# Products with a recurrent state on four tiles of TensorE at once, and a new written-out order

## The chip, the core and the metric

The kernel runs on one core of a Trainium2 chip. Its engines work side by side, each through its own queue in order: TensorE (PE; its weight loads stand apart as PEld), VectorE (DVE), ScalarE (ACT), GpSimd (POOL), and SyncE (SP), which issues nearly all DMAs. The metric is device time in microseconds: the median of three runs. A profiled execution is a further one, and has a time of its own.

## The reference

A linear attention with decay, then two MLP blocks, for 2 batches, 8 heads of 48 and 768 tokens:

```python
for t in range(S):
    cur = np.einsum('bhd,bhe->bhde', u[None] * kt, vt)
    y[:, :, t] = np.einsum('bhd,bhde->bhe', rt, state + cur)
    state = wt[:, :, :, None] * state + np.einsum('bhd,bhe->bhde', kt, vt)

h = gelu(x @ w_in);  u, v = split(h);  v_n = layernorm(v) * g_ln
x = x + (u * (w_sg @ v_n + b_sg)) @ w_out

xk, xr = mixes of x and x of the token before, by mu_k and mu_r
out = sigmoid(xr @ w_r) * (relu(xk @ w_k) ** 2 @ w_v)
```

The weights of the MLPs come as 64-bit floats.

## The kernel before

**Attention.** The recurrence is cut into chunks of 64 tokens. A *unit* is one batch, one half of the sequence (384 tokens, six chunks) and one pair of heads: 16 units, of which 0 to 3 and 8 to 11 are first halves of the sequence. A pair's heads lie on partitions 0 to 47 and 64 to 111. Per unit the code makes, in this order as the data needs it:

- `scores` (token A, line 346) and `sums` (P, 354) into `pA`; `turn` (T, 333), a transpose of the keys, and `keys` (k, 337 and 339), which copies them back;
- `weigh` (m, 385) and `now` (n, 391) on VectorE: masked scores and the part of the current token;
- `states` (S, 363) into `pkv`, and `fade` (x): ScalarE copies them to `kv` (373), VectorE runs a scan over the chunks into `sx` (377);
- `inner` (J, 400) and `inject` (N, 406) into `py`, then `outer` (I, 413), the products of `r` with the states, into the same `py`;
- `store` (O, 418 or 421): ScalarE copies `py` to `xT`, or to `t1` for the last pair, which `share` (o) spreads by DMA.

These products have a depth of 64 or 48 and 64 or 48 columns, a quarter of TensorE's array. Which quarter a product takes follows from the partitions of its operands (the row half) and of its output (the column half). The loops run over `QUAD`, head h and parity q of the chunk, in the order (0,0), (1,1), (0,1), (1,0). In `scores` the row half goes with h and the column half with q; in `states`, `inner` and `inject` the other way round, so each set of four has four different quarters. In `outer` both go with h: there are two quarters for four products. Each of these products is of type f32 and stands as two rows in the trace. The tiles `pA` and `pkv` share one buffer, and `py` has one.

The states of a unit lie in `sx` as `[112, 48, 7]`, chunk last, so that one state's 48 columns are seven words apart; a second half's first state comes as a packed copy, `sl` (380).

**MLP.** Products of full size in three terms of high and low parts (`mm3`, lines 209 to 211): v, u, M, W, E, R, Z in the order, with `xsplit` (X), `gate` (G) and `mix` (Y) between. Weights (tokens C) are converted by VectorE in three integer steps (156, 161, 165) and split by ScalarE (168) and VectorE (177). `packs` (L, D, j, g, d, K, f) prepare decays on VectorE (271 to 288).

**Order.** Nothing is scheduled by a program: `ORDER` is a text of tokens, and each issues its instructions on all queues at once, DMAs too. Token e (line 654) issues a product that computes nothing, "idle". The attention ends at token `|`.

Of the kernel before, what the change touches and what calls it, by code (L numbers as in the profile page):

```python
# [43 lines left out]
n5 g5 C1.o d5 C1.q C2.h k5 O4 S5.0 J5 N5 S5.1 S5.2 e x5.0 K5 T6 A6 I5 P6 o3 o3 o3 C3.l w6 63 64 w7 65 X0.1.h X0.2.h C2.r X0.0.h C2.q O5 f5 k6 X0.2.l
C3.x C2.o C4.x v0.2 n6 m6 C3.b X0.1.l S6.0 S6.1 J6 N6 S6.2 X0.0.l C3.t C4.b L6 x6.0 D6 T7 v0.1 A7 P7 I6 C4.r v0.2 C3.h C3.o C4.t C4.q k7 v0.1 C3.r O6
C4.h C3.q C5.l m7 C5.x n7 C5.b C5.t j6 w8 q6 C5.h v0.0 S7.0 S7.1 J7 N7 S7.2 C4.o C5.o u0.0 u0.3 g6 K6 d6 C6.l C6.h x7.0 v0.2 q7 C15.l C15.h w9 L7 u0.0
f6 L8 q8 A8 P8 I7 D7 m8 n8 j7 g7 K7 d7 T8 O7 k8 C5.r v0.2 u0.3 J8 N8 S8.0 S8.1 S8.2 x8.0 u0.1 T9 A9 P9 I8 u0.2 o7 o7 o7 q10 67 C7.l w10 v0.0 v0.1 v0.0
O8 k9 D8 C6.o m9 j8 n9 g8 K8 X1.0.h X1.0.l d8 C15.o S9.0 J9 S9.1 N9 S9.2 X1.1.h v1.0 f7 X1.1.l x9.0 T10 A10 P10 I9 X1.2.h C7.h u0.2 v0.1 C5.q v0.0
v0.0 O9 n10 L9 D9 m10 C7.o X1.2.l j9 g9 v0.0 q9 d9 C8.l 68 66 v1.1 k10 u0.1 f8 v0.1 C8.h v0.2 S10.0 J10 S10.1 N10 S10.2 x10.0 v0.2 f9 v1.0 u1.1 T11
A11 P11 I10 w11 n11 K9 m11 v0.1 k11 v1.1 O10 L10 w12 B v1.0 v1.1 u1.3 J11 N11 S11.0 S11.1 S11.2 D10 j10 x11.0 g10 d10 L11 C11.l C9.l C11.h v1.0 v1.0  # L50
v1.0 K10 v1.2 A12 I11 P12 T12 v1.2 O11 C9.h u1.1 k12 u1.2 u1.2 v1.1 v1.1 m12 C11.o n12 C8.o J12 S12.0 S12.1 N12 S12.2 C13.l w13 C10.l q11 x12.0 u1.0
T13 A13 P13 I12 v1.2 C10.h v1.2 C9.o D11 n13 v1.1 O12 v1.2 u1.0 k13 j11 C10.o m13 v1.2 o11 g11 C24.l C24.x K11 M0.3 M0.3 J13 S13.0 N13 S13.1 S13.2
M0.0 o11 o11 X2.2.h X2.2.l x13.0 d11 X2.0.h C16.l C16.h C13.h C16.o M0.0 M0.0 C13.o A14 P14 I13 T14 w14 C19.l M0.3 n14 M0.2 w15 610 69 O13 X2.1.h k14
X2.1.l X2.0.l C19.x m14 C19.r C19.q C17.l 611 J14 N14 S14.0 S14.1 S14.2 C19.b C19.t M0.2 x14.0 v2.1 T15 I14 A15 P15 C14.l C14.h C14.o n15 m15 C24.r
f11 O14 k15 f10 v2.1 C17.h C24.q v2.0 J15 S15.0 N15 S15.1 S15.2 M0.1 C24.b C17.o C24.t M0.2 C12.l C12.h C12.o x15.0 M0.1 I15 v2.1 v2.2 C21.l O15 C21.r
u1.3 C21.q v2.2 v2.1 v2.0 | C19.h C24.h M1.0 M1.0 M1.0 C24.o M1.3 M1.2 v2.0 C20.l C18.l C18.r C18.q C19.o C21.x C20.x C20.b M0.1 C20.t C20.h C20.o
C21.b M1.1 C21.t C21.h v2.2 C18.x M1.3 C21.o C18.b C18.t C18.h M1.2 M1.2 C18.o M1.1 v2.0 v2.0 v2.1 v2.0 u2.0 u2.0 G0.0.h C25.l v2.1 C25.x G0.0.l C25.b
v2.2 C26.l C26.x o15 o15 o15 u2.1 u2.1 v2.2 G0.1.h v2.2 C20.r G0.2.h u2.3 u2.2 C22.l G0.3.h G0.1.l M1.1 C26.b G0.2.l u2.2 X3.0.h C20.q X3.2.h u2.3
G0.3.l C25.t W0.0 W0.0 C26.t X3.0.l C25.h C25.o X3.1.h C22.x C22.b X3.1.l C26.r C26.q C22.r C22.q W0.1 C25.r C26.h v3.0 W0.2 C22.t W0.1 X3.2.l W0.2
C26.o C34.l C27.l v3.0 v3.0 C25.q v3.2 C22.h v3.2 v3.1 M1.3 C27.x u3.1 v3.2 C35.l v3.0 v3.0 v3.1 u3.1 u3.3 u3.0 u3.2 v3.1 C27.b C27.t C27.h v3.2 C22.o  # L60
v3.2 C34.x C34.b u3.3 v3.0 v3.2 C27.o C34.t v3.1 C34.r C28.l G1.2.h u3.0 v3.1 v3.1 C34.q G1.0.h u3.2 C34.h C27.r C27.q C35.x C35.b M2.3 G1.2.l M2.3
C35.t C35.h C35.o M2.2 M2.2 M2.2 C31.l C28.r G1.3.h G1.3.l C28.q M2.1 M2.0 C31.r G1.1.h G1.0.l G1.1.l C31.q C35.r C34.o C31.x C31.b C31.t C35.q C31.h
M2.3 C28.x C28.b C28.t C28.h M2.0 C31.o W1.1 M2.1 C23.l C29.l C36.l W1.1 M2.0 M2.1 C28.o C29.x C29.b W1.2 W1.0 W1.0 G2.1.h G2.0.h F C29.r C29.q C29.t
C23.x C23.b C29.h C23.t C23.h C23.o C36.x C37.l M3.0 M3.1 G2.3.h C36.r C36.q C37.r M3.0 G2.3.l G2.0.l C29.o M3.1 C37.x C37.q G2.2.h G2.2.l M3.0 M3.1
C37.b M3.3 M3.2 M3.3 H0 G2.1.l Y0.0.0.a W1.2 M3.2 Y0.0.2.a Y0.0.1.a Y0.1.1.a M3.3 C36.b C37.t C37.h Y0.0.0.b Y0.0.1.b W2.2 W2.2 W2.0 W2.1 Y0.0.2.b
Y0.1.0.a C36.t G3.0.h C23.r Y0.1.0.b C23.q Y0.1.1.b Y0.0.0.c Y0.0.2.c Y0.0.1.c C37.o W2.1 W2.0 C38.l C38.x C30.l C32.l E0.1 G3.3.h M3.2 Y0.1.0.c E0.0
E0.0 E0.1 C38.b C38.t E0.1 E0.2 C38.h C36.h C38.r C38.o E0.0 E0.0 E0.1 E0.1 E0.0 E0.3 E0.3 E0.2 C36.o E0.6 Z0.0 C33.l Y0.1.2.a E0.2 Y0.1.2.b C33.x
Y0.1.2.c Y0.1.1.c C30.x C30.b C30.t C33.b E0.2 C30.h E0.3 E0.3 C38.q E0.2 C33.t E0.3 E0.6 E0.6 E0.6 C30.o C32.x G3.3.l E0.5 R0.0 Z0.1 E0.4 E0.4 E0.4
E0.4 E0.7 G3.1.h C32.b C32.t C32.h C33.h C32.r C32.q Z0.2 R0.2 Z0.3 E0.4 E0.6 C33.o C32.o Z0.4 E0.7 E0.5 E0.5 R0.0 H1 Y1.0.0.a Y1.0.0.b E0.5 Y1.0.1.a
E0.5 Y1.0.0.c Y1.0.2.a E0.7 R0.1 R0.1 Z0.5 Z0.6 Y1.1.0.a Y1.0.1.b Y1.0.1.c C30.r Y1.1.0.b E0.7 Y1.0.2.b Y1.0.2.c E1.0 E1.0 C30.q Y1.1.1.a E0.7 E1.0  # L70
G3.1.l G3.0.l Y1.1.2.a C33.r C33.q G3.2.h E1.2 E1.2 Y1.1.1.b Y1.1.2.b R0.2 Z0.7 z0.0 E1.0 Y1.1.1.c E1.2 E1.2 E1.2 E1.4 E1.5 E1.1 E1.5 G3.2.l Y1.1.2.c
E1.0 Y1.1.0.c E1.5 E1.3 E1.5 E1.3 H2 E1.5 z0.1 E1.3 z0.2 E1.1 Y2.0.0.a E1.1 E1.3 E1.1 E1.1 y0.0 y0.2 y0.1 R1.1 R1.0 E1.4 E1.4 E1.4 E1.4 E1.6 E1.6 R1.0
R1.2 W3.1 Z1.0 E1.7 E1.3 W3.1 Y2.0.0.b Y2.0.0.c E1.6 Y2.0.2.a Y2.0.1.a Y2.1.1.a Y2.1.0.a R1.2 E1.7 Y2.1.0.b Y2.0.1.b Y2.0.2.b E1.6 R1.1 E1.7 E1.7
Y2.0.1.c W3.0 Z1.1 Z1.2 Z1.3 Z1.4 Y2.1.0.c E1.6 Y2.1.2.a Y2.1.2.b E1.7 Y2.1.1.b Y2.1.2.c Z1.5 Z1.6 Y2.1.1.c Y2.0.2.c E2.0 E2.0 E2.2 E2.2 E2.2 E2.0
W3.0 E2.3 Z1.7 E2.0 z1.1 E2.0 E2.3 E2.3 z1.2 E2.3 z1.0 W3.2 W3.2 E2.3 E2.5 E2.1 E2.1 E2.2 E2.2 E2.4 E2.5 E2.5 E2.1 E2.1 E2.5 H3 Y3.0.0.a Y3.0.2.a E2.5
y1.2 y1.0 y1.1 R2.0 E2.6 E2.7 E2.6 E2.6 E2.1 E2.4 E2.6 E2.6 Y3.0.0.b Y3.0.2.b E2.7 Y3.0.1.a E2.7 Y3.0.1.b Y3.0.1.c E2.4 Y3.1.2.a Y3.0.0.c R2.2 Z2.0
E2.7 R2.0 R2.2 E2.4 E2.4 Z2.1 Z2.2 Z2.3 Z2.4 Z2.5 Y3.1.0.a Y3.0.2.c Y3.1.1.a E3.1 R2.1 E3.0 Y3.1.0.b E3.0 Y3.1.1.b E3.2 Z2.6 Y3.1.1.c E2.7 E3.3 E3.0
Z2.7 E3.3 E3.3 E3.0 z2.0 R2.1 E3.3 E3.6 E3.0 Y3.1.0.c Y3.1.2.b z2.1 Y3.1.2.c R3.1 E3.3 E3.2 E3.2 E3.2 E3.1 E3.1 E3.1 z2.2 E3.2 E3.1 y2.0 y2.2 y2.1
E3.5 E3.4 R3.0 E3.4 E3.6 E3.4 E3.6 E3.6 E3.4 R3.0 E3.4 R3.2 R3.2 E3.5 E3.6 R3.1 E3.5 E3.5 E3.5 E3.7 E3.7 E3.7 E3.7 E3.7 Z3.0 Z3.2 z3.2 z3.0 Z3.1 y3.2
# [853 lines left out]
```

## Time and profile before

| | |
|---|---|
| median of 3 runs | 335.76 us (335.6 to 336.11) |
| profiled execution | 336.34 us, its span 334.4 us |
| TensorE, weight loads | 319.8 us (96%), 296.3 us (89%) |
| VectorE, ScalarE, GpSimd | 239.5, 182.3, 44.3 us |
| instructions | 8994 |
| HBM over the span | 81 GB/s |

The span is the time from the first to the last instruction that the profiler saw. Busy shares are sums over the whole span, which has stages of different kinds. Ends of matmuls are modelled and overlap the next ones, so what a group of products costs is read from its start to the start of the next group, its slot. "issue" names time in which an engine waited for nothing that the profile shows.

### The profile page before, as it was taken

How to read it: one execution, taken by the hardware profiler on the slowest of the kernel's cores; microseconds unless marked ns; L12 is line 12 of the kernel's file. 1: busy time of each engine (PE TensorE's matmuls, PEld its weight loads, DVE VectorE, ACT ScalarE, POOL GpSimd, SP SyncE). 2: the span in 40 equal slices, each digit the busy share in tenths (PEclk: the TensorE clock that was granted, in tenths of full speed). 3: DMA queues.
4: the chain of work that ended last, by engine and by line, in shares of the span. 5: the costliest groups of instructions: out<-in, count | busy, mean ns of one | idle time of the engine just before them, and what ended most of it. 6: DMA issues, size and time to landing. Idle time of an engine off the chain costs nothing.

```text
span 334.4 us, 8994 instructions
## 1 busy us (share of the span) xinstructions
PE 319.8 (96%) x3734; PEld 296.3 (89%) x3734; DVE 239.5 (72%) x451; ACT 182.3 (54%) x432; POOL 44.3 (13%) x98
## 2 busy tenths in 40 slices
...
GB/s 207 233 211 142 100 222 163 146 143 168 119 153 93 162 149 20 70 136 156 4 95 159 47 0 144 47 2 0 25 49 0 0 2 71 2 0 24 49 0 76
DMA packets 16509, 30.00 MB, mean 90 GB/s; under 512 B 2256, under 2 KB 12496, under 8 KB 16464
## 3 DMA queue, kind: packets, MB, share of 16 engines
...
q14 instruction: 15, 0.12, 0.1%
...
## 4 chain that ended last, share of the span: by engine, by line
PE 78%; DMA 4%; DVE 2%; ACT 2%; SPq 2%; issue 1%; DVEq 0%; ACTq 0%
PE po L575 11%; PE pk L210 5%; PE pk L209 5%; PE pk L211 5%; PE ps L209 5%; PE ps L211 5%; PE ps L210 5%; PE po L211 4%; PE po L210 4%; PE po L209 4%; PE pu L209 2%; PE py L413 2%; PE pu L211 2%; PE pu L210 2%; PE pv L209 2%; PE pr L211 2%
## 5 line engine op out<-in xcount | busy, mean ns | idle before, releaser
L209 PE MATMUL ps<-wsg,vn_hi 128*128 128x384 f32 x96 | 32.7, 340 | 0.0
L210 PE MATMUL pk<-xk_lo,wk_hi 128*128 128x384 f32 x96 | 32.6, 339 | 0.0
L211 PE MATMUL ps<-wsg,vn_lo 128*128 128x384 f32 x96 | 32.4, 337 | 0.1
L209 PE MATMUL pk<-xk_hi,wk_hi 128*128 128x384 f32 x96 | 32.5, 338 | 0.0
L211 PE MATMUL pk<-xk_hi,wk_lo 128*128 128x384 f32 x96 | 32.4, 338 | 0.0
L210 PE MATMUL ps<-wsg,vn_hi 128*128 128x384 f32 x96 | 32.3, 336 | 0.0
L547 ACT ACTIVATE kr<-pk 128x384 f32<-128x384 f32 x32 | 15.3, 490 | 26.4 <-PE pk L211 20.0
L549 DVE TENSOR_TENSOR kr<-kr 128x384 f32<-128x384 f32 x32 | 17.5, 555 | 16.0 <-ACT kr L547 15.8
L556 DVE TENSOR_TENSOR kk_lo<-kr,kk_hi 128x384 fp32r<-128x384 f32 x32 | 17.3, 554 | 9.3 <-ACT kk_hi L554 9.3
L554 ACT CAST kk_hi<-kr 128x384 fp32r<-128x384 f32 x32 | 16.0, 511 | 14.3 <-DVE kr L549 10.9
L575 PE MATMUL po<-pl_win_hi,kk_hi 128*128 128x384 f32 x81 | 22.8, 336 | 0.0
L377 DVE TENSOR_TENSOR_SCAN sx<-kv,fd 112x336 f32<-112x336 f32 x16 | 13.7, 855 | 7.8 <-ACT kv L373 7.3
L211 PEld LDWEIGHTS ps<-wsg,vn_lo 128*128 128x128 f32 x96 | 18.0, 188 | 0.4 <-DVE vn_lo L479 0.4
L209 PEld LDWEIGHTS ps<-wsg,vn_hi 128*128 128x128 f32 x96 | 18.0, 188 | 0.3
L575 PE MATMUL po<-pl_win_lo,kk_hi 128*128 128x384 f32 x63 | 18.2, 336 | 0.0
L210 PEld LDWEIGHTS pk<-xk_lo,wk_hi 128*128 128x128 f32 x96 | 18.0, 188 | 0.2 <-DVE xk_lo L538 0.2
L575 PE MATMUL po<-pl_win_hi,kk_lo 128*128 128x384 f32 x54 | 18.2, 337 | 0.0
L209 PEld LDWEIGHTS pk<-xk_hi,wk_hi 128*128 128x128 f32 x96 | 18.0, 188 | 0.1
L210 PEld LDWEIGHTS ps<-wsg,vn_hi 128*128 128x128 f32 x96 | 18.1, 188 | 0.0
L211 PEld LDWEIGHTS pk<-xk_hi,wk_lo 128*128 128x128 f32 x96 | 18.0, 188 | 0.0
L209 PE MATMUL pu<-xs_hi,win_hi 128*128 128x384 f32 x48 | 16.8, 351 | 0.0
L211 PE MATMUL po<-ga_hi,wout_lo 128*128 128x384 f32 x48 | 16.2, 337 | 0.0
...
## 6 DMA issues: line engine op xcount, KB each, us to landing
...
wsg_raw<-in_w_sgT_dram SPq DMA_DIRECT2D x12, 192.0 KB, 3.0
out_dram<-rr SPq DMA_DIRECT2D x12, 192.0 KB, 1.9
...
```

The lines of the kernel that those rows point to most:

```text
L209: T.matmul(ps, lh, rh, start=(i == 0), stop=False)
L210: T.matmul(ps, lh, rl, start=False, stop=False)
L211: T.matmul(ps, ll, rh, start=False, stop=(i == n - 1))
L377: V.tensor_tensor_scan(u.sx.rearrange(flat), u.kv.rearrange(flat), u.fd.rearrange(flat), 0.0, ALU.add, ALU.mult)
L413: T.matmul(u.py[o:o + D, q, c * CA:(c + 1) * CA], u.state(n)[o:o + D, :], u.rp[o:o + D, n * CA:(n + 1) * CA], start=False, stop=(c == NCB ...
L547: A.activation(kr, ps, AF.Relu)
L549: V.tensor_mul(kr, kr, kr)
L554: A.copy(hi, kr)
L556: V.tensor_sub(lo, kr, hi.bitcast(F32))
L575: T.matmul(pv[g][s], l, wv[i][r], start=st, stop=(i == KF - 1 and l is ll))
```

## The change

Outputs of `inner`, `inject` and `outer` go to the column half `h ^ q` in place of h. Chunks of odd parity so stand in the other half of `py`'s partitions, and the four products of `outer` take four different quarters; `inner` and `inject` keep four. `store` becomes three copies: even chunks of both heads (112 x 192), and odd chunks of each head (48 x 192) with the halves exchanged. `ORDER` is new throughout; it has 68 idle tokens in place of 44, 57 of them ahead of unit 7's states in place of 44, two ahead of unit 10's `turn`, and nine behind the last product of all.

```diff
-... L2 q2 C0.l w1 g1 m0 n0 T0 e J0 k0 N0 S0.0 S0.1 S0.2 f1 d1 D2
+... L2 w1 C0.l q2 e T0 e e e e J0 k0 S0.0 S0.1 N0 S0.2 e e d1 D2 x0.0
...
         def inner(u):
             for c in range(NCB):
                 for h, q in QUAD:
                     o, t, m = 64 * h, 64 * q, (64, D)[h]
-                    T.matmul(u.py[o:o + m, q, c * CA:(c + 1) * CA], u.vk[t:t + 64, c, h * D:h * D + m], u.am[t:t + 64, h, c * CA:(c + 1) * CA], start=(c == 0), stop=False)
+                    y = 64 * (h ^ q)
+                    T.matmul(u.py[y:y + m, q, c * CA:(c + 1) * CA], u.vk[t:t + 64, c, h * D:h * D + m], u.am[t:t + 64, h, c * CA:(c + 1) * CA], start=(c == 0), stop=False)

         def outer(u):
             for c in range(NCB):
                 for h, q in QUAD:
-                    n, o = 2 * c + q, 64 * h
+                    n, o, y = 2 * c + q, 64 * h, 64 * (h ^ q)
                     if u.state(n) is not None:
-                        T.matmul(u.py[o:o + D, q, c * CA:(c + 1) * CA], u.state(n)[o:o + D, :], u.rp[o:o + D, n * CA:(n + 1) * CA], start=False, stop=(c == NCB - 1))
+                        T.matmul(u.py[y:y + D, q, c * CA:(c + 1) * CA], u.state(n)[o:o + D, :], u.rp[o:o + D, n * CA:(n + 1) * CA], start=False, stop=(c == NCB - 1))

         def store(u):
-            y = u.py[:R, :, :NCB * CA].rearrange("r q (c t) -> r c q t", c=NCB)
             if u.p < NP - 1:
-                A.copy(xT[u.g][:R, u.p, 1:].rearrange("r (c q t) -> r c q t", c=NCB, q=2), y)
-                return
-            u.t1 = shp.tile([R, TB], F32, name=f"t1_{u.n}", tag="t1")
-            A.copy(u.t1.rearrange("r (c q t) -> r c q t", c=NCB, q=2), y)
+                x = xT[u.g][:, u.p, 1:]
+            else:
+                x = u.t1 = shp.tile([R, TB], F32, name=f"t1_{u.n}", tag="t1")
+            x = x.rearrange("r (c q t) -> r q c t", c=NCB, q=2)
+            y = u.py[:, :, :NCB * CA].rearrange("r q (c t) -> r q c t", c=NCB)
+            A.copy(x[:R, 0], y[:R, 0])
+            for h in range(2):
+                o, z = 64 * h, 64 - 64 * h
+                A.copy(x[o:o + D, 1], y[z:z + D, 1])
```

`inject` is changed as `inner` is. The lines behind `inner` move: `inner` is 401, `outer` 415, `store` 424 and 427, idle products 660, the flag's product 690.

How the order moves instructions shows at three places. The first is TensorE's queue around the outer of unit 2 (`py_0_2`), near 28 us, before (names carry batch, half and pair; the last number counts tiles):

```order
L363 MATMUL pkv_0_2_589<-vk_0_2_389,kT_0_2_542 48x48
L346 MATMUL pA_1_0_614<-pk_0_426 64x64 x12
L354 MATMUL pA_1_0_614<-c_sb,pk_0_426 64x1 x12
L413 MATMUL py_0_2_564<-pk_2_377,sx_0_2_590 48x64 x10
L654 LDWEIGHTS d1pat
L654 MATMUL idle<-d1pat 128x512
L654 LDWEIGHTS d1pat
L654 MATMUL idle<-d1pat 128x512
L400 MATMUL py_0_3_665<-am_0_3_533,vk_0_3_537 64x64
```

The same place of the change:

```order
L333 MATMUL ptr_0_3_575<-c_sb,six 128x112 x3
L346 MATMUL pA_0_3_579<-six 64x64 x12
L354 MATMUL pA_0_3_579<-c_sb,six 64x1 x12
L415 MATMUL py_0_2_527<-pk_2_342,sx_0_2_522 48x64 x10
L660 LDWEIGHTS d1pat
L660 MATMUL idle<-d1pat 128x512
L660 LDWEIGHTS d1pat
L660 MATMUL idle<-d1pat 128x512
L660 LDWEIGHTS d1pat
L660 MATMUL idle<-d1pat 128x512
L401 MATMUL py_0_3_649<-am_0_3_634,vk_0_3_622 64x64
```

Before, the scores of unit 4 (`pA_1_0`) stand ahead of unit 2's outer, and those of unit 3 further up; now it is unit 3's scores that stand there, unit 4's come after unit 3's states, and three idle products stand in place of two.

The second is ScalarE's queue around the store of unit 4 (`py_1_0`), before:

```order
L337 COPY kT_1_1_852<-ptr_1_1_795 128x336
L339 COPY fd_141<-pk_1_654 112x48x6
L418 COPY xT_84<-py_1_0_758 112x384
L373 COPY kv_143<-pkv_1_1_856 112x48x6
L445 CAST xs_hi<-xT_83 128x3x128 x2
```

The same place of the change:

```order
L183 ACTIVATE winv_512_q<-winv_512_raw 128x512
L131 ACTIVATE winv_512_q,flags<-winv_512_q,lim_q 128x512
L424 COPY xT_84<-py_1_0_768 112x3x64
L427 COPY xT_84<-py_1_0_768 48x3x64 x2
L337 COPY kT_1_1_881<-ptr_1_1_857 128x336
L339 COPY fd_141<-pk_1_637 112x48x6
L373 COPY kv_143<-pkv_1_1_926 112x48x6
L451 CAST xs_hi<-xT_83 128x3x128 x3
```

Three copies stand in place of one, and they now go ahead of unit 5's key copies, which stood ahead of the store.

The third is the end of TensorE's queue, before, with the last product of the last output block and the flag's product:

```order
L209 MATMUL po_3_1_4336<-pl_win_hi,kk_hi 128x384
L210 MATMUL po_3_1_4336<-pl_win_lo,kk_hi 128x384
L211 MATMUL po_3_1_4336<-pl_win_hi,kk_lo 128x384
L684 MATMUL pf<-ones,fl 1x1
```

The same place of the change:

```order
L209 MATMUL po_3_2_4398<-pl_win_hi,kk_hi 128x384
L210 MATMUL po_3_2_4398<-pl_win_lo,kk_hi 128x384
L211 MATMUL po_3_2_4398<-pl_win_hi,kk_lo 128x384
L660 LDWEIGHTS d1pat
L660 MATMUL idle<-d1pat 128x512
...
L690 MATMUL pf<-ones,fl 1x1
```

Nine idle products, of which one is shown, now stand between the last product and the flag's.

## Rows read from the trace of the kernel before

**Rows 1.** The page, busy time and its share of the span, with instructions.
```profile
PE 319.8 (96%) x3734; PEld 296.3 (89%) x3734; DVE 239.5 (72%) x451; ACT 182.3 (54%) x432; POOL 44.3 (13%) x98
```

**Rows 2.** Busy time by stretch: length, engines, granted clock, DMA share, GB/s.
```profile
0.00:45.60 45.60, 38.24 (x961) 26.96 (x961) 36.40 (x63) 20.63 (x51) 10.94 (x40) 0.93 0.61 183
45.60:126.30 80.70, 78.05 (x1624) 68.25 (x1620) 65.09 (x118) 54.61 (x138) 21.84 (x37) 1.00 0.53 148
126.30:329.50 203.20, 203.20 (x1154) 201.04 (x1152) 137.21 (x267) 107.03 (x245) 11.51 (x21) 1.00 0.15 47
```

**Rows 3.** Timeline of TensorE in two stretches: start, length, engine, line, operation.
```profile
52.64 0.58 PE L346 MATMUL pA<-six 48*64 48x64 f32 x24
53.04 0.48 PE L354 MATMUL pA<-c_sb,six 48*64 48x1 f32 x24
53.36 0.23 PE L413 MATMUL py<-pk,sl 48*48 48x64 f32 x1
...
54.48 0.50 PE L209 MATMUL pv<-win_hi,xs_hi 128*128 128x512 f32 x1
...
67.75 1.08 PE L413 MATMUL py<-pk,sx 48*48 48x64 f32 x20
68.75 0.45 PE L209 MATMUL pu<-xs_hi,win_hi 128*128 128x384 f32 x1
```

**Rows 4.** Line 413, weight loads: ns least/median/most, first and last start.
```profile
L413 PEld LDWEIGHTS py<-pk,sx x240: 158/181/200, 14.3 to 117.4; 48*48 48x48 f32 x120
...
L413 PEld LDWEIGHTS py<-pk,sl x24: 116/122/138, 39.3 to 116.8; 48*48 48x48 f32 x24
```

**Rows 5.** VectorE's groups by form: busy, mean ns, idle before.
```profile
L276 DVE RECIPROCAL d1w<-sc 128x6 f32<-128x6 f32 x12 | 2.2, 182 | 0.1
...
L165 DVE SCALAR_TENSOR_TENSOR winu_x<-winu_raw,winu_x 128x512 int32<-128x512 int32 x3 | 2.1, 687 | 0.0
L161 DVE SCALAR_TENSOR_TENSOR winu_x<-winu_raw,winu_x 128x512 int32<-128x512 int32 x3 | 2.0, 682 | 0.0
...
L156 DVE TENSOR_SCALAR winu_x<-winu_raw 128x512 int32<-128x512 int32 x3 | 1.3, 423 | 1.3 <-DMA winu_raw<-in_w_in_dram 1.3
```

**Rows 6.** Timeline of TensorE and VectorE near 27 us; a stretch at half clock.
```profile
26.81 0.56 PE L363 MATMUL pkv<-vk,kT 64*64 64x48 f32 x23 [2.12 <-issue]
27.86 0.86 DVE L377 TENSOR_TENSOR_SCAN sx<-kv,fd 112x336 f32<-112x336 f32 x1 [2.13 <-ACT kv L373]
33.81 0.86 DVE L377 TENSOR_TENSOR_SCAN sx<-kv,fd 112x336 f32<-112x336 f32 x1 [1.80 <-ACT kv L373]
28.30:35.10 6.80, 6.80 (x143) 4.95 (x135) 5.00 (x10) 2.37 (x6) 1.62 (x3) 0.50 0.78 243
```

**Rows 7.** Timeline of TensorE, five idle products and what follows.
```profile
11.30 1.25 PE L654 MATMUL idle<-d1pat 128*128 128x512 bf16 x5
12.48 0.58 PE L346 MATMUL pA<-pk 48*64 48x64 f32 x24
```

**Rows 8.** ScalarE's groups by form, the copies out of PSUM.
```profile
L373 ACT COPY kv<-pkv 112x288 f32<-112x288 f32 x16 | 6.4, 400 | 15.6 <-PE pkv L363 15.6
L418 ACT COPY xT<-py 112x384 f32<-112x384 f32 x12 | 5.7, 478 | 8.3 <-PE py L413 8.3
```

**Rows 9.** What line 400 waited for from 45.6 us on: us, times.
```profile
  ACT wout_q L183: 1.0, 2
  ACT wsg L168: 0.4, 1
  ACT t L421: 0.4, 1
  ACT vj L467: 0.2, 1
```

**Rows 10.** Timeline of the end.
```profile
329.16 0.34 PE L210 MATMUL po<-pl_win_lo,kk_hi 128*128 128x384 f32 x1
...
329.33 0.34 PE L211 MATMUL po<-pl_win_hi,kk_lo 128*128 128x384 f32 x1
...
330.30 0.33 SPq L583 DMA_DIRECT2D out_dram<-rr  x1
...
330.45 0.19 PE L684 MATMUL pf<-ones,fl 128*1 128x1 f32 x2 [0.78 <-DVE fl L681]
330.68 0.14 DVE L685 TENSOR_SCALAR fi<-pf 1x1 int32<-1x1 f32 x1 [0.28 <-PE pf L684]
```

**Rows 11.** DMA issues: count, KB each, median us to landing.
```profile
out_dram<-rr SPq DMA_DIRECT2D x12, 192.0 KB, 1.9
```

More of the change, by code (lines that the diff above doesn't have):

```diff
@@ L44 @@
[L44 to L79, printed above, removed]
@@ new lines @@
+e e C3.l w5 q5 C2.t j5 C2.r C2.q O4 k5 o3 m5 n5 C4.l L6 o3 o3 g5 C1.o d5 K5 J5 N5 S5.0 S5.1 S5.2 e e x5.0 e T6 A6 P6 I5 X0.0.h X0.1.h X0.2.h C2.h w6
+63 w7 C5.l 65 64 q6 X0.1.l C4.x C2.o m6 C4.b C3.r C3.q O5 f5 k6 n6 C4.t v0.1 X0.2.l C4.h D6 C4.o C3.x J6 N6 S6.0 S6.1 S6.2 v0.2 x6.0 T7 I6 A7 P7 C5.x
+X0.0.l C3.b C5.b j6 m7 v0.0 C4.r k7 O6 C4.q v0.2 v0.1 n7 C3.t C3.h C5.t g6 C3.o C5.h C5.o d6 S7.0 S7.1 J7 N7 S7.2 u0.1 x7.0 T8 K6 A8 I7 P8 v0.1 L7 q7
+B C13.l w8 C13.h C11.l f6 C5.r C5.q u0.1 O7 u0.0 u0.2 L8 q8 w9 o7 C8.l o7 o7 D7 m8 j7 g7 d7 n8 K7 k8 S8.0 S8.1 J8 N8 S8.2 u0.0 C11.h v0.1 v0.0 f7 D8
@@ new lines @@
+j8 K8 C13.o x8.0 g8 u0.3 T9 A9 P9 I8 v0.0 v0.2 X1.0.h X1.2.h C8.h k9 X1.0.l C6.l w10 O8 v0.0 X1.1.h C8.o X1.2.l n9 m9 v1.0 S9.0 S9.1 J9 N9 S9.2 d8 L9
+C6.h u0.2 D9 C6.o x9.0 67 C12.l 66 68 q9 e e T10 v0.0 v0.1 A10 P10 I9 u0.3 f8 O9 k10 C11.o j9 g9 n10 v1.2 v0.0 m10 X1.1.l S10.0 S10.1 J10 N10 S10.2
+v1.1 T11 v0.1 K9 v1.0 x10.0 I10 A11 P11 C12.h C10.l C10.h v0.2 v1.2 v0.2 C10.o d9 L10 D10 v0.2 f9 k11 w11 w12 C7.l O10 n11 m11 j10 C17.l L11 q10 u1.1
+S11.0 J11 N11 S11.1 S11.2 v1.0 v1.2 T12 u1.0 x11.0 K10 C17.h C17.o C12.o A12 I11 P12 n12 m12 g10 v1.0 u1.1 d10 k12 v1.1 v1.0 O11 u1.2 v1.2 C7.h C7.o
@@ new lines @@
+u1.2 S12.0 S12.1 J12 N12 S12.2 x12.0 v1.0 v1.1 u1.3 T13 I12 A13 P13 C9.l C9.h u1.0 v1.2 v1.1 v1.1 D11 C9.o j11 v1.1 v1.2 g11 M0.1 q11 M0.1 w13 o11 o11
+69 M0.1 K11 m13 n13 d11 M0.3 610 o11 C14.l k13 O12 u1.3 C15.l C15.h C14.h C14.o J13 N13 S13.0 S13.1 S13.2 C15.o x13.0 M0.0 T14 w14 C16.l A14 I13 P14
+k14 C16.h C16.o M0.3 C24.l C24.x C24.b C20.l 611 w15 C19.l O13 C24.r X2.0.h X2.2.h X2.1.h X2.1.l M1.3 m14 C24.t n14 v2.1 C24.q v2.1 S14.0 J14 S14.1
+N14 S14.2 x14.0 X2.2.l C20.x C18.l T15 M1.0 A15 I14 P15 X2.0.l M1.3 v2.2 n15 m15 M0.3 M0.0 M0.0 M1.3 C20.b C20.t C18.r C18.q k15 f11 O14 C20.r C20.q
@@ new lines @@
+C19.r v2.2 S15.0 S15.1 J15 N15 S15.2 x15.0 M1.0 v2.0 I15 v2.2 v2.1 f10 O15 | C24.h C20.h v2.1 v2.0 C19.q M1.1 M0.2 M1.2 v2.0 C20.o C18.x C24.o M1.0
+C19.x C19.b C18.b C18.t M1.1 C19.t C19.h M0.2 M0.2 C19.o o15 C21.l G0.3.h G0.3.l C21.x C26.l o15 M1.2 C21.b v2.0 C18.h C18.o v2.0 v2.2 v2.2 v2.2 v2.1
+M1.1 v2.1 C21.t u2.1 u2.1 C21.r o15 C25.l C22.l u2.2 C21.q G0.0.h u2.2 v2.0 u2.3 u2.0 C21.h G0.2.h G0.1.h G0.0.l C26.x C21.o G0.1.l u2.0 G0.2.l X3.0.h
+u2.3 X3.1.h W0.0 C26.b C25.x X3.0.l C26.t X3.1.l C22.r C26.h C22.q C25.b W0.0 C26.o W0.2 C22.x X3.2.h C26.r C22.b C22.t C22.h C26.q W0.2 C25.t v3.0
@@ new lines @@
+W0.1 W0.1 X3.2.l C25.r v3.0 C25.h C25.o C34.l C35.l C23.l v3.0 v3.1 v3.1 G1.3.h v3.1 v3.2 u3.3 C23.x C23.b v3.0 v3.2 u3.3 C23.t u3.1 u3.0 u3.2 v3.2
+v3.1 C23.h v3.0 v3.0 C22.o u3.0 v3.1 v3.2 v3.2 C25.q u3.1 C34.r C23.o v3.1 C35.x C35.b v3.2 C34.x C34.b C34.t M2.1 M2.2 M1.2 G1.1.h C34.h G1.0.h C34.q
+G1.1.l C35.t C35.h C35.r C35.q M2.1 C34.o M2.2 C35.o G1.3.l C27.l C36.l C27.x C27.b M2.2 C27.t G1.2.h C23.r G1.2.l C23.q u3.2 M2.0 M3.3 C36.x C27.r
+C27.h C27.q C27.o C36.b G1.0.l C36.t M3.3 M2.3 C29.l C36.h C36.o M2.1 C29.x C29.b C28.l M3.3 C29.t M2.3 C36.r C36.q W1.0 W1.2 C28.x C28.b M2.0 C28.t
@@ new lines @@
+C28.r C28.q C30.l C30.r C28.h C29.h C37.l W1.2 W1.1 C28.o M3.0 C30.x G2.1.h G2.2.h C30.q C30.b M2.0 M2.3 G2.2.l C29.o W1.0 G2.1.l G2.0.h G2.0.l M3.0
+C37.x C37.b C37.t M3.0 C37.r C37.q C30.t W1.1 C29.r M3.1 M3.2 C32.l C38.l C31.l M3.1 H0 Y0.0.0.a Y0.0.1.a G2.3.h Y0.0.2.a G2.3.l M3.2 C37.h Y0.0.0.b
+C29.q Y0.0.0.c M3.1 Y0.0.2.b Y0.0.1.b W2.2 W2.1 C37.o Y0.1.1.a Y0.0.2.c Y0.0.1.c W2.1 C38.x Y0.1.0.a E0.0 E0.0 C38.b Y0.1.0.b Y0.1.1.b M3.2 E0.0 W2.2
+E0.0 Y0.1.1.c E0.0 E0.2 E0.2 C38.t C38.h C38.o E0.1 E0.7 E0.1 C30.h F E0.1 C31.x E0.2 Y0.1.2.a Y0.1.2.b E0.1 C30.o Y0.1.0.c E0.1 Y0.1.2.c E0.7 E0.7
```

24 lines of the change are left out of this document (18 added, 6 removed).

## The prediction

> **What bounds the kernel now.** I read the busy shares first, then stretches, then the rows of the steps that the change touches. The page gives TensorE 96% of the span, VectorE 72%, ScalarE 54% [rows 1], but three stretches hide in this average [rows 2]. Up to 45.6 us TensorE is busy 38.24 of 45.60, part of it with products that compute nothing: "idle" products from order token e, 44 in the program. Real work is scarce there: VectorE, busy 36.40, must first make decays, scores and converted weights. From 45.6 us, the first `pv` product, to 126.3 us TensorE is busy 78.05 of 80.70 with attention and MLP products interleaved. From there to 329.5 it is never idle. So a product removed before 45.6 us is worth nothing by itself; one removed behind it is worth its slot, as long as the other engines keep up.
>
> **The products with the state.** In the stretch between, unit 6's twelve products at L413 start at 53.36 us and `pv` follows at 54.48: a slot of 1.12 us for 24 rows (an f32 product is two). Units 0 to 3 and 8 to 11 have ten products, as one has no state before its first chunk: 20 rows, 67.75 to 68.75, 1.00 us. The scores at L346, with the same depth and columns but four tiles at once, take 52.64 to 53.04, 0.40 us for 24 rows [rows 3]. So 0.40 is one end; the other is 1.12, nothing gained. It could not be much worse than that, since pairs that ran at once before still may. Why isn't 1.12 just twice 0.40? The weight loads differ: the median load from `sx` (a state's columns stand seven words apart) is 181 ns, from the packed copy `sl` 122 ns, and the four extra rows with `sl` lengthen a slot by 0.12 us where twenty with `sx` take 1.00 [rows 3, 4]. The products with `sx` are thus held by their loads, some 0.1 us per load in each row half, and the change doesn't touch these. If two column halves load side by side, half a slot is left: 0.56 and 0.50. I take 0.62 and 0.55, a tenth over half, because the change to the next shape of tile at either end isn't halved.
>
> [...]
>
> In both orders seven units (0 to 6) have their outer ahead of unit 7's states, in the part where VectorE sets the pace, so I count nothing for them. Nine follow: units 7 and 12 to 15 save 0.50 each, units 8 to 11 save 0.45. That is 5 x 0.50 + 4 x 0.45 = 4.3 us saved. Both ends: 9 x 0 = 0, and at the scores' price (0.40, and 0.33 for 20 rows) 5 x 0.72 + 4 x 0.67 = 6.3.
>
> **What the new order does at the start.** Up to unit 7's states TensorE has the same real products in both orders (three `pv` among them), but 13 more idle ones. VectorE's work up to unit 7's weighing grows by two instructions: a reciprocal of 0.18 us and a first conversion step of about 0.42, with one second step in place of a third, both 0.68: +0.6 us [rows 5]. [...] In the new order unit 3's scores stand ahead of unit 2's outer, unit 4's go behind unit 3's states, and idle products fill the places. [...] I take -1.6, nearer to the hole alone going, and not the whole of it. With +0.6 the start is worth -1.0 us.
>
> **Idle products later.** Two new ones stand ahead of unit 10's turn, where TensorE is otherwise full: five take 11.30 to 12.48 us, 0.236 each [rows 7], so +0.5 us; 0 if it waits there anyway.
>
> **The copy back.** One copy of 112 x 384 becomes one of 112 x 192 and two of 48 x 192. The trace has none of 192; 384 takes 0.48 us and 288 takes 0.40 [rows 8], so 96 elements cost 0.08 and I put 0.32 on one of 192 (an estimate from these): 0.96 in place of 0.48, about 0.5 us longer per unit, 8 us over 16 units. The second copy waits for the first besides. Nor does any row show ScalarE writing to other partitions than it reads; I take the same price. ScalarE is busy 54.61 of 80.70 in the stretch [rows 2], so there is room in the sum. What counts is the wait behind it: `py` has one buffer, so the next unit's inner products wait for the last copy, and all MLP products behind them in the queue. Behind 45.6 us L400's weight load waited for such a copy at one place, 0.4 us for L421 [rows 9]; elsewhere MLP products stand between and cover the copy. One place uncovered: +0.5 us; all nine uncovered: +4.5; all covered: 0.
>
> **The tail.** Nine idle products stand behind the last real one, ahead of the flag product `pf` in TensorE's queue. In before the last product starts at 329.33 and `pf` at 330.45, when VectorE is ready; at 330.68 VectorE makes of it the flag that every engine reads to choose its branch [rows 10]. Products of this size follow each other by 0.17 us, so nine by 0.236 from 329.50 end at 331.62, and `pf` comes 1.2 us later. If the end hangs on the flag, +1.2; if it hangs on the last output's DMA, issued at 330.30 and landing 1.9 us later, at 332.2 [rows 10, 11], nothing. I take +1.2: no engine can leave before it has the flag, and that is made 3.7 us ahead of the span's end.
>
> **Sum.** -4.3 - 1.0 + 0.5 + 0.5 + 1.2 = -3.1 us. The profiled execution took 336.34, so 333.2; it stands 0.6 above the median of the runs, 335.76, and against that I predict 332.7.
>
> **Rivals.**
> First, the products gain nothing: two column halves of one row half read the same partitions, and 0.1 us per strided load may be what these partitions deliver, not what a tile can take. Then four at a time load as slowly as two, all waste of the new order remains, and the time is 332.7 + 4.3 = 337.0, slower than before; it decides as soon as the slots stay above 0.9 us. For it speaks that loads, not columns, hold the slot [rows 4]; against it, that the scores load from both column halves within 0.40 us. [...]
> [...]
> Second, the copies set the pace: if all nine later units wait 0.5 us at `py` instead of one, 332.7 + 4.0 = 336.7. Against it: one place of 0.4 us in all of before's stretch [rows 9].
> [...]
> [...]
>
> **Numbers.** Forecast 0.40, its own range 330.5 to 335; products gain nothing 0.27; copies 0.07; start worse 0.12; all good 0.14. A difference under 0.2% (0.7 us) can hardly be told from none here. Faster: 0.14, nearly all of the forecast's 0.40, and a little of the rivals where a gain at the start meets them: 0.55. Same, from the edges of forecast and of the rivals that end near 336: 0.10. Slower: 0.35. Eight in ten lie from 328.2 to 338.5.
>
> **What would show it.** L415's slots of 24 rows at 0.62 us (0.9 or more: first rival). `pv` starting about 1 us earlier than 45.6; no "issue" gap near 2 us and no stretch at half clock ahead of it. Three copies of some 0.3 us per unit, with inner products behind 45.6 us waiting for them at one place or none. `pf` starting 2.3 us behind the last product, not 1.1. TensorE as full as before from unit 7 on; if it shows more than 3 us of idle time there, VectorE or ScalarE didn't keep up and I am wrong on what the stretch hangs on.

## The result, and the profile after

The changed kernel took 331.75 us (median of 4 runs, 330.78 to 333.16), the kernel before 335.72 beside it: a ratio of 0.9883 with a 95% interval of 0.9845 to 0.9921, so 1.2% or 4.0 us faster. I had predicted 332.7. Its profiled execution took 330.78, span 328.9; that is at the fast end of its runs, and 5.5 us of span under the profiled execution of before. In later measurements both kernels were 1 to 2 us slower and their runs spread over 4 to 5 us, so below only ratios to the kernel before, run on the same chip, are compared, and stretches of profiles. One run of the experiments fell into a slower state and is left out.

The page of the changed kernel, as in [rows 1], and the granted clock over the span:
```profile
PE 316.9 (96%) x3752; PEld 290.4 (88%) x3758; DVE 239.6 (73%) x451; ACT 190.5 (58%) x464; POOL 36.2 (11%) x98
...
PEclk9999999999999999999999999999999999999999
```
ScalarE has 8.2 us more, as counted (16 x 0.5). The clock row is whole in every slice; before had a stretch of 0.50 [rows 6].

Busy time by stretch, cut where [rows 2] are cut (start to first `pv` product, to the end of unit 15's products with the state, to the last product), with the same columns:
```profile
0.00:43.57 43.57, 35.98 (x969) 23.67 (x974) 36.56 (x65) 23.34 (x61) 8.37 (x40) 1.00 0.69 199
43.57:124.80 81.23, 80.45 (x1650) 69.50 (x1648) 65.91 (x120) 63.42 (x166) 17.88 (x38) 1.00 0.49 139
124.80:323.10 198.30, 198.30 (x1128) 196.36 (x1125) 136.31 (x265) 103.70 (x238) 9.91 (x21) 1.00 0.15 50
```
The first is 2.0 us shorter. The second is no shorter, but holds more: 1650 products against 1624. Two of them are idle products; the others are big MLP products that the new order brought forward from the third stretch, where they are missing. TensorE's idle time in it fell from 2.65 to 0.78 us.

The products with the state, in the timeline of TensorE: ten on the upper two rows, twelve on the lower three. They answer to the last four of [rows 3].
```profile
66.21 0.74 PE L415 MATMUL py<-pk,sx 48*48 48x64 f32 x20
66.88 0.50 PE L209 MATMUL pv<-win_hi,xs_hi 128*128 128x512 f32 x1
...
124.12 0.25 PE L415 MATMUL py<-six,sl 48*48 48x64 f32 x1
...
124.80 0.44 PE L209 MATMUL ps<-wsg,vn_hi 128*128 128x384 f32 x1
```
From the first start to the next tile's first start the slots are 0.67 and 0.68 us, where before had 1.00 and 1.12. (124.12 is unit 15, whose first products read `sl`.)

The end, answering to [rows 10]:
```profile
322.93 0.34 PE L211 MATMUL po<-pl_win_hi,kk_lo 128*128 128x384 f32 x1
...
323.33 1.89 PE L660 MATMUL idle<-d1pat 128*128 128x512 bf16 x8
...
323.96 0.33 SPq L589 DMA_DIRECT2D out_dram<-rr  x1
325.15 0.09 PEld L690 LDWEIGHTS pf<-ones,fl 128*1 128x1 f32 x2 [0.42 <-PE idle L660]
...
325.38 0.15 DVE L691 TENSOR_SCALAR fi<-pf 1x1 int32<-1x1 f32 x1 [1.32 <-PE pf L690]
```
`pf` starts 2.22 us behind the last product, in before 1.12, and what it waits for is named: the idle products. The span ends 5.97 us behind the start of the last product, in before 334.4 - 329.33 = 5.07.

### The profile page after: what moved, and what is told of

It reads as the page before. It is cut to its first block, busy times and chain, and to the rows that moved or that the text cites. A ratio compares the mean times of both kernels' runs of the same rounds, so it can differ in the third digit from the quotient of the medians.

```text
span 328.9 us, 9073 instructions
## 1 busy us (share of the span) xinstructions
PE 316.9 (96%) x3752; PEld 290.4 (88%) x3758; DVE 239.6 (73%) x451; ACT 190.5 (58%) x464; POOL 36.2 (11%) x98
## 3 DMA queue, kind: packets, MB, share of 16 engines
HBM read 24.65 MB, written 2.36 MB: 82 GB/s over the span
## 4 chain that ended last, share of the span: by engine, by line
PE 82%; ACT 9%; issue 2%; DVE 1%; DMA 1%; SPq 1%; POOL 1%; ACTq 0%; DVEq 0%; POOLq 0%
PE po L581 11%; PE pk L210 5%; PE pk L209 5%; PE pk L211 5%; PE ps L209 5%; PE ps L211 5%; PE ps L210 5%; PE po L211 4%; PE po L210 4%; PE po L209 4%; PE pv L209 2%; PE idle L660 2%; PE pv L210 2%; PE pv L211 2%; PE py L415 2%
## 5 line engine op out<-in xcount | busy, mean ns | idle before, releaser
L660 PE MATMUL idle<-d1pat 128*128 128x512 bf16 x62 | 18.4, 406 | 2.3 <-POOL lim_tanh L121 1.4
L584 DVE TENSOR_TENSOR rr<-po,rr 128x384 f32<-128x384 f32 x12 | 6.6, 554 | 17.7 <-PE po L211 8.4
```

What stands on the lines that cost most here:

```text
L584: V.tensor_mul(rr[g][:, s, :], pv[g][s], rr[g][:, s, :])
L660: T.matmul(ps_d.tile([P, 512], F32, name="idle", tag="d"), d[:, :P], d[:, :512], start=True, stop=True)
```

## The experiments

Each kernel ran beside the kernel before. "Unit 7's states" is the start of that unit's L363 products, from where on TensorE has enough to do; it is at 56.77 us in the profile of before and at 53.44 in that of the changed kernel.

### Layout alone, order alone

```diff
-ORDER = """L0 D0 j0 e e q0 e e e e e e e e e e e Q L1 w0 q1 g0 f0 d0 K0 A0 P0 D1 n0 j1 m0 g1 K1 L2 w1 C0.l q2 e T0 e e e e J0 k0
...
+ORDER = """e L0 D0 j0 g0 q0 L1 d0 D1 f0 e e e e e e e e e e e e e e e e q1 K0 j1 K1 e e e Q A0 P0 w0 L2 q2 C0.l w1 g1 m0 n0 T0 e J0 k0
...
```
(the changed kernel with the order of before; the second run is the kernel before with the new order, the same diff the other way round)

> The new column halves and the three copies with the order of before. Theory 1, the layout carries its own gain: the slots of the products with the state fall as in the changed kernel's trace, from 1.12 to about 0.71 us (24 rows) and from 1.00 to about 0.67 (20 rows), so the nine units behind unit 7's states save 5 x 0.41 + 4 x 0.33 = 3.4 us, the copies give 0.5 back, and the median is about 332.8. The start keeps its stop of about 2 us at 25 us and its stretch at half clock. Rival, the order carries the gain and the layout needs it (with the old order inner products wait for the last of three copies): 335 or more, with waits of L401 for L427 behind 45 us at several places.

> The old column halves and the one copy with the new order. Theory 1, the start's gain is the order's: the first pv product starts about 2 us earlier than 45.6 and unit 7's states about 3 us earlier than 56.8, with no half clock; the two idle products and the tail give back 0.5 and 1.0, so the median is 335.7 - 3.3 + 1.5 = 333.9, slots of the products with the state at 1.0 and 1.12 us. Rival, the start is shorter because the products with the state and the copies are shorter there: the start is as long as before, and the time is 335.7 + 1.5 = 337.2.

Measured: layout alone 337.94 us (12 runs), ratio 1.0036 (1.0006 to 1.0067); order alone 335.86 (12 runs), ratio 0.9966 (0.9932 to 0.9999). Neither makes the gain; together they make 1.2%. For the layout alone the rival was right: nothing is gained, though its slots are as short (0.67 for ten products, 0.70 to 0.78 for twelve). For the order alone the rival's time (337.2, a ratio of 1.0045) is out, and theory 1's (333.9, 0.9946) lies inside the interval; but theory 1's mechanism is not in its profile, which has unit 7's states at 57.14, no earlier than before, with a stretch of half clock (columns: stretch, length, TensorE busy, granted clock, DMA share, GB/s):
```profile
32.00:34.00 2.00, 2.00 (x23) 0.50 0.24 85
```
That is one profile, and it took 0.9 us more than the median of these runs.

Where the layout's slots went is in what TensorE waited for between unit 7's states and unit 15's products with the state, and in the busy time of that stretch. Layout alone (line; us in total, times, longest):
```profile
PE pkv L363 <- ACT kT L337: 1.8, 1, 1.8
PE ps L209 <- ACT vn_hi L483: 1.2, 1, 1.2
PE py L401 <- ACT t L427: 1.1, 1, 1.1
PE py L401 <- DVE am L385: 1.0, 1, 1.0
PE pv L209 <- ACT uT L491: 0.5, 1, 0.5
PE pu L209 <- ACT v L469: 0.4, 1, 0.4
```
```profile
54.26:124.33 70.07, 63.90 (x1422) 56.21 (x1422) 54.69 (x98) 51.34 (x135) 19.62 (x35) 1.00 0.49 136
```
The changed kernel:
```profile
PE pkv L363 <- DVE am L385: 0.3, 1, 0.3
PE idle L660 <- ACT uT L491: 0.2, 1, 0.2
```
```profile
53.44:124.12 70.68, 69.91 (x1452) 61.13 (x1451) 55.94 (x100) 54.82 (x143) 16.76 (x35) 1.00 0.44 123
```
With the old order TensorE is idle for 70.07 - 63.90 = 6.17 us (in the fastest of the twelve runs, 2.7 us under their median, so the profile shows the waits but not the whole loss), and five of the six waits are for ScalarE: one for a copy at L427 itself, four for other work in ScalarE's queue. Whether the copies make that work late is the next question. In the kernel before the same stretch (56.77 to 125.12) has 1.89 us idle. The new order has 0.77.

### One copy instead of three, in both orders

```diff
-            x = x.rearrange("r (c q t) -> r q c t", c=NCB, q=2)
-            y = u.py[:, :, :NCB * CA].rearrange("r q (c t) -> r q c t", c=NCB)
-            A.copy(x[:R, 0], y[:R, 0])
-            for h in range(2):
-                o, z = 64 * h, 64 - 64 * h
-                A.copy(x[o:o + D, 1], y[z:z + D, 1])
+            x = x.rearrange("r (c q t) -> r c q t", c=NCB, q=2)
+            A.copy(x[:R], u.py[:R, :, :NCB * CA].rearrange("r q (c t) -> r c q t", c=NCB))
...
```
(the line of `inner` that gives one product in four its 16 more columns is left out)

> The column halves with the order of before, and one copy of 112 x 384 in place of three; the halves are not exchanged, so odd chunks of 64 tokens land in the wrong rows, and one product in four of the inner ones takes 16 columns more so that all rows are written. Theory 1, ScalarE's longer copies ate the layout's gain (idle time of TensorE from 60 to 126 us rose from 1.9 to 6.2 us, inner products waiting for L427 and others for ScalarE's work behind it): with one copy the waits fall back to about 2 us and the time is about 3.5 us under the layout alone, 334.5 against 337.9, or 2 under before. Rival, with its slots shorter TensorE merely comes sooner to work that VectorE and ScalarE finish when they did: the idle time stays above 5 us and the time within 1 us of the layout alone.

> The changed kernel (new order) with one copy of 112 x 384 in place of three; the halves are not exchanged, and one inner product in four takes 16 columns more, as in the run with the old order. Theory 1, the new order makes room for the longer copies: behind 45 us TensorE waits for L427 at one place and ahead of it three times by 0.25 to 0.37 us, so one copy is worth 0.5 to 1.5 us against the changed kernel (ratio to before 0.984 to 0.987), where it was worth 5.3 us in the old order. Rival, the copies cost as much in any order, since ScalarE is late in every unit: 4 to 5 us, ratio about 0.974.

Measured: in the old order 333.61 us (6 runs), ratio 0.9878 (0.9846 to 0.9910), against 1.0036 with three copies: the three copies cost 1.6%, some 5 us. In the new order 332.79 (12 runs), ratio 0.9899 (0.9867 to 0.9932), against 0.9885 (0.9849 to 0.9921) for the changed kernel run again: nothing that these intervals, some 1.1 us to either side, can tell. Both rivals are out. Theory 1's sizes are not right: in the old order one copy is worth 5 us where it had 3.5, in the new order its 0.5 to 1.5 us are not seen. With one copy the old order waits about as much as before did (first row and stretch):
```profile
PE pkv L363 <- ACT kT L337: 1.1, 1, 1.1
```
```profile
56.44:122.67 66.23, 63.97 (x1422) 56.02 (x1422) 53.79 (x98) 46.41 (x116) 20.03 (x35) 1.00 0.52 140
```
66.23 - 63.97 = 2.26 us idle, 3.9 us less than with three copies. So the copies are why layout and order need each other: the same 8 us of ScalarE are dear in one order and cost nothing that shows in the other. And with one copy the layout gains as much in the old order (0.9878) as the whole change does (0.9885): room for the three copies is what the new order brings, and nothing else of it shows beyond these intervals.

### What holds a slot: weights from neighbouring words

```diff
-            return u.sx[:, :, c - 1]
+            return u.sx.rearrange("r e n -> r (e n)")[:, (c - 1) * D:c * D]
```
(the first run in the changed kernel, the second in the kernel before)

> The changed kernel, with the products with the state reading their weights from 48 neighbouring words of the same tile instead of every seventh word (so other states than the right ones are read; all else, waits too, is as in the changed kernel). Theory 1, strided loads hold these slots even four at a time: loads fall from 181 to about 120 ns, the slots from 0.67 to about 0.40 us, and the nine units behind unit 7's states save 9 x 0.28 = 2.5 us, so about 329.2. [...]

> The kernel before, its products with the state reading their weights from 48 neighbouring words in place of every seventh (other states than the right ones are read). It has two of these products at a time, where the changed kernel with the same edit has four. Theory 1, loads hold the slot in both layouts and column halves load side by side: 24 rows take about twice the 0.48 us of four at a time, 0.85 to 0.96, 20 rows about 0.9. Rival, in this layout the loads are hidden and the 64 columns hold the slot: 24 rows stay at 1.1, 20 rows at 1.0.

Measured: 331.22 us (6 runs), ratio 0.9846 (0.9811 to 0.9882) in the changed kernel; 334.92, one run, in the kernel before. Theory 1's 2.5 us in the changed kernel are not seen: the ratio is 0.4%, or 1.3 us, under the changed kernel's, and the intervals overlap. It is the slots that decide. Loads and ten-product slots, four at a time and strided (the changed kernel; its slot is above), then four at a time and packed, then two at a time and packed:
```profile
L415 PEld LDWEIGHTS py<-pk,sx x240: 158/182/192, 13.3 to 117.9; 48*48 48x48 f32 x120
```
```profile
L415 PEld LDWEIGHTS py<-pk,sx x240: 116/120/201, 13.3 to 120.1; 48*48 48x48 f32 x120
```
```profile
32.83 0.54 PE L415 MATMUL py<-six,sx 48*48 48x64 f32 x20
33.30 0.39 PE L660 MATMUL idle<-d1pat 128*128 128x512 bf16 x1
```
```profile
L413 PEld LDWEIGHTS py<-pk,sx x240: 116/120/200, 14.3 to 116.2; 48*48 48x48 f32 x120
```
```profile
66.82 0.74 PE L413 MATMUL py<-pk,sx 48*48 48x64 f32 x20
67.49 0.44 PE L209 MATMUL pu<-xs_hi,win_hi 128*128 128x384 f32 x1
```
Strided: 1.00 two at a time, 0.67 four at a time. Packed: 0.67 and 0.47. Slots of twelve products are 1.12 and 0.68 strided, 0.79 (97.38 to 98.17) and 0.49 (126.32 to 126.81) packed. So loads hold the slot in both layouts (theory 1, though the four packed ones save 0.20 us, not 0.27, and the two packed ones come out under its 0.85 to 0.96), and going from two to four tiles takes a slot to 0.61 to 0.70 of its length, not to half of it. In the kernel before, packed weights alone would have given the ten-product slots that the new layout has, without three copies; but the scan writes them at a stride, and another copy would have to pack them, which wasn't tried.

### The idle products

```diff
-Z3.1 z3.1 z3.0 Z3.2 y3.0 y3.1 e e e e e e e e e R3.2 z3.2 y3.2"""
+Z3.1 z3.1 z3.0 Z3.2 y3.0 y3.1 R3.2 z3.2 y3.2"""
```
(the first run; the second leaves out the two ahead of T10 besides; the third has those, and leaves out the 57 ahead of unit 7's states instead)

> The changed kernel without its nine last idle products. Theory 1, the end hangs on the flag: the flag product follows VectorE's sum by 0.1 us as in the kernel before, and the time falls by 1.0 us, to about 330.7. Rival, the end hangs on the last output's transfer, which lands at 325.8 whether or not the flag waits: the time stays within 0.3 us of the changed kernel's, about 331.7.

> The changed kernel without its eleven last idle products, the nine of the end and the two ahead of unit 10's turn. Theory 1, both are on the path: 0.8 us for the end (5.97 us from the last product's start to the span's end with them, 5.18 without) and 0.5 to 0.65 for the two (0.65 is their slot in the changed kernel's trace), so 1.3 to 1.5 us under the changed kernel run beside it. Rival, the two fill a wait of unit 10's turn for its operands, so only 0.8 is gained.

> The changed kernel without the 57 idle products ahead of unit 7's states; all else stands in the same order. Theory 1, VectorE sets the pace there and the idle products cost nothing, as I counted: but they keep TensorE at its full granted clock; without them stretches of 0.50 appear between 5 and 50 us, and the time is 1 to 4 us longer. Rival, they are in the way (they make TensorE fetch 114 instructions more and stand ahead of real products): unit 7's states start earlier than with them and the time is the same or 1 to 2 us shorter.

Measured: without the nine 332.55 us (5 runs, ratio 0.9867, 0.9818 to 0.9915), without eleven 333.37 (6 runs, 0.9891, 0.9867 to 0.9916): neither can be told from the changed kernel (0.9885). In their profiles the end is shorter, 5.18 and 5.15 us from the last product's start in place of 5.97, so 0.8 us, where theory 1 had 1.0 and then 0.8; the times don't resolve it. The two ahead of T10 cost nothing that shows: from unit 7's states to unit 15's products with the state it is 71.62 us without them, and 70.68, 71.62 and 71.66 with them (the changed kernel, the profile without the nine, and the changed kernel's second). But the rival's reason is not the one in the trace. Without the two, unit 10's turn starts 0.24 us after the last states (72.08 and 72.32) and waits for nothing; with them it is 1.1 to 1.3 us. What is gained there is waited for a little later, at unit 9's products with the state, for VectorE's scan and at "issue"; the `pv` product behind them starts 20.97 us after unit 7's states, and 20.98 in the changed kernel's second profile. The waits of the run without eleven:
```profile
PE py L415 <- issue: 0.4, 1, 0.4
PE py L415 <- DVE sx L377: 0.3, 1, 0.3
```

Without the 57 early ones the time is 336.70 (13 runs), ratio 0.9992 (0.9971 to 1.0012): nearly the whole gain of the change is gone, about 3 us (the changed kernel had 333.82 on the same chip). Theory 1 holds in the time, and in its mechanism too, though the row of the granted clock says 1.00. TensorE from 5 to 35 us without them (one group and the stretch):
```profile
L346 PE MATMUL pA<-pk 48*64 48x64 f32 x96 | 3.7, 320 | 8.3 <-DVE pk L284 6.7 <-ACT kv L373 1.6
```
```profile
5.00:35.00 30.00, 23.08 (x623) 20.06 (x623) 25.76 (x45) 13.67 (x39) 4.18 (x12) 1.00 0.76 219
```
and with them, in the changed kernel's second profile, the same scores at a granted clock of 0.99 (5 to 28 us) and then of 0.50 (28 to 36 us):
```profile
L346 PE MATMUL pA<-pk 48*64 48x64 f32 x72 | 1.8, 227 | 0.2 <-DVE pk L284 0.2
```
```profile
L346 PE MATMUL pA<-pk 48*64 48x64 f32 x24 | 1.2, 325 | 0.5 <-issue 0.5
```
A product of the scores takes 227 ns at full clock and 325 at half. Without idle products it takes 320, although the row says 1.00. That row counts time for which the trace holds no record of the clock as whole, and here the first record, of 1.00, begins at 44.93 us; in the changed kernel it begins at 4.15, in the kernel before at 4.38. The lengths of products change at that very time. The first row below is from 5 to 45 us, the second from 45 to 60:
```profile
L401 PE MATMUL py<-am,vk 64*64 64x64 f32 x72 | 5.5, 320 | 3.9 <-ACT xT L427 3.2 <-DVE am L385 0.4 <-ACT t L427 0.3
```
```profile
L401 PE MATMUL py<-am,vk 64*64 64x64 f32 x24 | 1.1, 223 | 0.0
```
In the changed kernel it is the first idle products that show the step, from 0 to 4.2 us and from 4.2 to 10:
```profile
L660 PE MATMUL idle<-d1pat 128*128 128x512 bf16 x7 | 3.0, 606 | 1.4 <-POOL lim_tanh L121 1.4
```
```profile
L660 PE MATMUL idle<-d1pat 128*128 128x512 bf16 x12 | 3.2, 387 | 0.0
```
So, read from these lengths, TensorE runs at the lower level up to 45 us without the early idle products, and from 4 us on at the upper one with them, outside the stretches of 0.50. That this makes the whole 3 us is argued: the profile without them is the fastest of its runs, 2.1 us under their median, and has unit 7's states at 56.15, as late as the slowest start with idle products and no later.

### The start, again

> The changed kernel itself, word for word, beside the others of this call. Theory 1, what moves its start from one execution to the next are TensorE's stops where a block of 256 of its instructions begins: each such stop ends 2.2 to 2.5 us after a 16 KB instruction transfer begins, unit 7's states start anywhere from 53.4 us (the first profile) to 55.6 (the profile without the last idle products, whose program is the same until then), and the single times spread over 2 to 3 us about 332. Rival, 53.4 is what the program does and the later starts were the other kernels' own: unit 7's states again at 53.4 within 0.5 us.

> The kernel before itself, for a second profile of its start. Theory 1, its start moves from one execution to the next as the changed kernel's does (53.4, 54.6 and 56.1 us in three profiles): unit 7's states start somewhere from 54.5 to 58.5, with stops of TensorE at other places than 24.6 us, each ending 2.2 to 2.5 us after a 16 KB instruction transfer begins. Rival, the 2.1 us stop at 24.6 us and unit 7's states at 56.8 belong to the program: both within 0.3 us of the first profile.

Measured: the changed kernel 333.82 us (6 runs, 331.18 to 335.32), ratio 0.9885 (0.9849 to 0.9921), as at first; the kernel before 336.70. For the changed kernel the rival is out: unit 7's states stand at 56.10 this time, half a microsecond beyond theory 1's own range, and the single times spread over 4.1 us. For before the rival holds in the start, 56.74, and in the place of the stop, at the same instruction, but not in its length (1.59 us, where it was 2.12 in [rows 6]); a stretch of half clock follows again:
```profile
26.12 0.56 PE L363 MATMUL pkv<-vk,kT 64*64 64x48 f32 x23 [1.59 <-issue]
```
```profile
26.80:34.10 7.30, 6.92 (x147) 5.29 (x147) 4.93 (x9) 2.45 (x6) 1.25 (x2) 0.53 0.70 208
```
Such stops didn't leave with the new order; the first profile of the changed kernel has two of about 1 us:
```profile
24.65 0.46 PE L354 MATMUL pA<-c_sb,six 48*64 48x1 f32 x20 [0.85 <-issue]
...
40.31 0.48 PE L408 MATMUL py<-c_sb,vg 64*64 64x64 f32 x18 [1.09 <-issue]
```
What goes with a later start is a half-clock stretch behind them. Four profiles have the same program up to there. The changed kernel: granted clock whole, unit 7's states at 53.44. Without eleven idle products: 0.57 from 27 to 31 us, 54.56. Without nine: a stretch like it, and ahead of it a wait of 1.58 us at 25 us, for the DMA of `six` and not at "issue", 55.63. The changed kernel again: 0.50 from 28 to 37 us, 56.10. The length of the stretch is not all: with the new order and one copy it is 0.71 from 26 to 31 us, and unit 7's states stand at 53.79.

## Why the prediction was right

The time was 0.95 us under the forecast and inside its own range of 330.5 to 335. Its terms, one by one:

**Products with the state: the mechanism right, the size a fifth too large.** I took 0.62 and 0.55 us for a slot, a tenth over half; measured are 0.68 and 0.67, or 0.61 and 0.67 of before's slots; the plain halves that I also gave, 0.56 and 0.50, are further off. By these nine units give 5 x 0.44 + 4 x 0.33 = 3.5 us, not 4.3. The first rival is out: slots above 0.9 would have been its sign. Row by row, the 20 of a ten-product slot start in before in pairs 6 to 9 ns apart, all within 0.83 us from 67.75 us on; in the changed kernel the first twelve start in fours, each within 60 ns, and all 20 within 0.49 us from 66.21 on. The change to the next shape, which I had named, is there in both: from the last row's start to that of the next tile's first product it is 180 ns. What else keeps a slot above half was not found. On the other side the count was one unit short: unit 6's products stand behind the first `pv` in both orders, where TensorE is already the bound, and I had put them into VectorE's part.

**Copies: 0.32 us each was right, the 0.5 us for one uncovered wait is not seen, and the reason is the order.** The rows are 0.320 for 112 x 192 and 0.315 for 48 x 192, also where ScalarE writes to other partitions than it reads. The second rival, copies setting the pace, had 0.07 from me; it is just what happens with this layout in the old order, where they cost 5 us. I read the cover from the old order's waits [rows 9] and got the new one's right by luck: those waits say what stood idle while TensorE was slower, not what would wait once it is quicker.

**Start: the sign right, the reason wrong.** No run shows the -1.6 us of the sum: it stood for a part of before's stop of 2.12 us and of the waits of 2.13 and 1.80 us behind it [rows 6]. The stops stayed, at other places (0.85 and 1.09 us in the changed kernel's first profile). What changed is that they don't always bring a half-clock stretch: unit 7's states came 0.6 to 3.3 us earlier in four profiles of that program, where I had 1.0. That the order does it is not shown: with the old layout its one profile gained nothing there (57.14), while the old order with the new layout came early in one (54.26) and hardly in another, with one copy (56.44). Nor did the "13 more idle ones" cost nothing just because they fill the places; the 57 together are worth about 3 us, and without them TensorE's products are 1.4 times as long up to 45 us.

**Two idle products ahead of unit 10: +0.5 forecast, 0 measured.** I had named that end, TensorE waiting there anyway; it waits not at the turn, but behind it, at unit 9's products with the state.

**Tail: +1.2 forecast, 0.8 to 0.9 measured in profiles**; `pf` stands 2.22 us behind the last product where I wrote 2.3. The rest is made up on the way to the end: from `fi` to the end it is 3.72 us in before and 3.5 in the changed kernel.

**TensorE as full as before from unit 7 on** held: from there to the last product 272.6 us became 269.5 (270.4 in the second profile), so 2.2 to 3.1 us for the three terms that I had put at -4.3 + 0.5 + 0.5 = -3.3. What the shorter slots give is partly waited for elsewhere: in the second profile TensorE is idle for 1.44 us between unit 7's states and unit 15's products with the state (0.5 for VectorE's `am`, 0.4 at "issue", 0.3 for ScalarE's `uT`), where order alone has 0.56. So that the sum is right to a microsecond is in part luck: the start gained more than I had in three of four profiles and the slots gained less, and the two errors offset each other.

Open: why layout alone and order alone differ from before by as little as they do (the first by waits, as shown; the second, 0.3%, was not taken apart), and how much of the 4 us is the start's: profiles of the same program differ there by 2.7 us. Nor was it tried whether packed weights in the new order, written without another copy, beat both kernels; of the versions run that compute the right output, none is faster than the changed kernel beyond the noise.
